# Storing the A22 forms with A11 and A12, and moving the first half's weight sums to one up block earlier

## The chip, the core and the metric

The kernel runs on one core of a Trainium2 chip. The metric is device time in microseconds (us) of the whole program; the time before is the median of three runs, 831.94 us (831.66 to 832.31). The engines are named as the profile names them: PE multiplies matrices, PEld is its weight load, DVE (VectorE) and POOL (GpSimd) do elementwise work, ACT (ScalarE) copies and scales, SP (SyncE) only issues transfers. POOL and ACT issue transfers too, each in the order of its own instruction stream.

## The reference

```python
def reference(q, k, v, w1, w2, w3, w_out):
    scores = scale * q @ k.T                      # per batch (8) and head (8), 576 x 64
    ret = (scores * Dmat) @ v                     # Dmat: gamma**(i-j) for i >= j, else 0
    x = ret.transpose(0, 2, 1, 3).reshape(4608, 512)
    a = x @ w1                                    # 512 x 1024
    b = x @ w2                                    # 512 x 1024
    h = a * b @ w3                                # 1024 x 1024
    return h @ w_out                              # 1024 x 512
```

Everything is float32 on the chip; the float64 inputs of the weights are converted in the kernel. `w3 @ w_out` is multiplied out once.

## The kernel before

**Tiling.** The 8 batches are taken in 4 pairs, each pair in 5 chunks of the sequence (one of 64 rows, four of 128), so there are 20 attention chunks `g`; `NC` is 5. An attention chunk costs PE the products `sc` (scores), `pm`-by-`ld_v` and `xps` and `st` (state). Its q and k come either as whole tiles that PE transposes (`tp`), or in 32 x 32 blocks: 16 small transfers for q and 16 for k (`load_blocks`, L171), a scaling of q on POOL (`scale_blocks`, L181), and block transposes on DVE (`front_blocks`, L190). The tokens are also cut into 12 blocks `m`, each of 2 x 192 tokens.

**Up blocks.** `up(i, n, fp)` multiplies one token block by one quarter `fp` of w1 and w2 with Strassen's seven products. Quarters 0 and 1 lie in half 0 of the weights (`wA[0]`, `wS[0]`), quarters 2 and 3 in half 1. An up block has 28 matmuls, four for each product, named here by its weight form: A11, S2, S3, S1, A22, then A12 added onto the bank of A11 (`p1`), then S4 added onto the bank of S1 (`p5`). DVE adds a product into the sum tile `c` in five calls of `plus` (L533): of S2, of S3, of `p5`, of A22, and of `p5` again after S4. The third of them has to have read `p5` before S4 may be added onto it. ACT copies `p1` into `c` at the start (L546) and once more later (L561); `c` has one buffer, so L546 of a block waits for L566, which multiplies the block before out of `c`. After its add, each `plus` takes one item off the list `aside` and then one off the list `spread` and runs them on the spot. So an item on `spread` stands on DVE between two of these adds.

**Weight forms.** From token block 4 on, `up2` uses a second level of Strassen on the weights. Each half `h` has 7 outer forms, each of which has 7 inner forms. In place on `wA[h]` and `wS[h]`, DVE makes the inner sums with two instructions each (L891: one on `wA` with 1024 columns, one on `wS` with 768): S3 in the place of A21; S2 = A22 - S3 in the place of A22; S1 = S2 + A11 in the place of A11; S4 = A12 - S2 in the place of A12. The forms are stored to `kept[h]` in device memory (`send`: L901 four transfers from `wA`, L904 one or L907 two from `wS`) and loaded again, one outer form at a time, into a ring for `up2` (`next_forms`, L961). A piece of `send` is named by its place `lo` in the 14 x 128 columns of a form, the column block `m`, and the row block `c` or `None` for both. A place may be overwritten only when its store has landed.

**Order before.** The instructions of each engine run in the order of the program text. `weight_forms(h, False)[2]()` at L1187 stores A11 and A12 on POOL's queue, at `g` = 5 for half 0 and at `g` = 6 for half 1. Then, from L1203, four up blocks of token block 3 and what stands between them are put on the list of work: up 0, up 1, `forms[0]` (S3 sum and store of S3 with A22 of half 0, on POOL's queue), up 2, `later` (two empty items), `forms[1]` (S2, S1, S4 sums and the store of S1, S4 and S2, on SP's queue), up 3, `flush`, `forms[2]` (S3 sum and store of S3 with A22 of half 1), `flush`, then the `down` blocks, which multiply `ab` by `w3 @ w_out`. A form entry extends `spread`; `flush` runs what is left on it. Up 0 and up 1 read `wA[0]`, up 2 and up 3 read `wA[1]`, which is why the sums of half 0 can be made from the end of up 1 on.

In this document, "up 0" to "up 3" are these four blocks, "down 1" is the `down` on blocks (1,0) and (1,1) that follows them, and "plus 1" to "plus 5" are the five L533 adds of a block in order. Before the change, the items run as follows: in up 2, plus 1 takes the S3 sum and plus 2 its store; in up 3, plus 1 takes `front_blocks` of q and an empty item, plus 2 an empty item, plus 3 `front_blocks` of k and the S2 sum, plus 4 a sum for `down` (L614) and the S1 sum, plus 5 another (L618) and the S4 sum; then come L566, the store of half 0 on SP, the S3 sum of half 1 and its store.

Of the kernel before, what the change touches and what calls it, by code (L numbers as in the profile page):

```python
# [13 lines left out]
ALU = mybir.AluOpType  # L14
# [5 lines left out]
def kernel(  # L20
# [20 lines left out]
    P = 128  # L41
# [16 lines left out]
    QC = CV // 2  # L58
# [28 lines left out]
    def load(g, names, engine=nc.sync):  # L87
        i, c = divmod(g, NC)
        sz = sizes[c]
        src = {"k": k, "q": q, "v": v}  # L90
        for nm in names:
            t = pools["ld"].tile([P, 2 * H, D], F32, tag="ld_" + nm, name="ld_" + nm)
            engine.dma_start(
                t[:sz], src[nm][2 * i:2 * i + 2, :, starts[c]:starts[c] + sz, :].rearrange("b h p d -> p (b h) d"))
            live[nm, g] = t
# [27 lines left out]
    for c in (0, slice(1, NC)):  # L123
        n = short if c == 0 else P
# [11 lines left out]
    wA = [wp.tile([P, 2, 2, KD // 2, CV], F32, tag=f"wA{h}", name="wA") for h in halves]  # L136
    wS = [wp.tile([P, 3, 2, 2, 2, P], F32, tag=f"wS{h}", name="wS") for h in halves]
# [22 lines left out]
    def load_blocks(g, nm):  # L160

        i, c = divmod(g, NC)
        n = sizes[c] // BL
        t = pools["ld"].tile([P, 2 * NP, P // BL, BL], F32, tag="ld_q", name="bl_" + nm)
        src = {"k": k, "q": q}[nm][2 * i:2 * i + 2].rearrange("b (p a) s d -> a (b p) s d", a=2)
        for a in range(2):
            for f in range(D // BL):
                part = (a * (D // BL) + f) * BL
                for m in range(n):
                    s0 = starts[c] + m * BL  # L170
                    nc.sync.dma_start(t[part:part + BL, :, m, :],  # L171
                                      src[a, :, s0:s0 + BL, f * BL:(f + 1) * BL].rearrange("m r x -> r m x"))
        live["bl_" + nm, g] = t
# [11 lines left out]
    def front_blocks(g, names="kq"):  # L185
        c = g % NC
        n = sizes[c] // BL
        for nm in names:
            dst = pools["fr"].tile([P, 2, NP, P], F32, tag=nm + "T", name=nm + "T", bufs=1 if nm == "k" else 2)
            nc.vector.transpose(  # L190
                dst[:, :, :, :sizes[c]].rearrange("p b m (n x) -> p (b m) n x", x=BL),
                live["bl_" + nm, g][:, :, :n, :])
            live[nm + "T", g] = dst

    def scale(g, nm, scalar=False, engine=nc.gpsimd):
        c = g % NC
        sz = sizes[c]
        t, gam = live[nm, g], {"q": gq, "v": gk}[nm]
        t = t[:sz].rearrange("p (b h) d -> p b h d", b=2)
        if scalar:  # L200
            for h in range(H) if scalar is True else scalar:
                nc.scalar.mul(t[:, :, h, :], t[:, :, h, :], gam[:sz, c, h:h + 1])
            return
        engine.tensor_tensor(
            out=t, in0=t, in1=gam[:sz, c].unsqueeze(1).unsqueeze(3).to_broadcast([sz, 2, H, D]), op=ALU.mult)

    def front(g, names="kq"):
        c = g % NC
        sz = sizes[c]
        for nm in names:  # L210
            src = live[nm, g]
            dst = pools["fr"].tile([P, 2, NP, P], F32, tag=nm + "T", name=nm + "T",
                                   bufs=1 if nm == "k" and g >= NC else 2)
            for b in range(2):
                tp = acc.tile([P, NP, P], F32, tag="acc", name="tp")
                for p in range(NP):
                    h = b * H + 2 * p
                    nc.tensor.transpose(tp[:, p, :sz],  # L218
                                        src[:sz, h:h + 2, :].rearrange("p a d -> p (a d)"),
                                        ident[:sz, :sz])  # L220
                nc.scalar.copy(dst[:, b, :, :sz], tp[:, :, :sz])
            live[nm + "T", g] = dst
# [349 lines left out]
    aside, owed, spread, beside, loads = [], [], [], [], []  # L572
# [256 lines left out]
    todo = [(0, 1, 2), (0, 0, 3), (0, 1, 3)] + [(0, 2, fp) for fp in range(NQ - 1)]  # L829
# [38 lines left out]
    todo = [(down, (0, 0), (0, 1)), (down, (0, 2), (1, 2))]  # L868
# [9 lines left out]
    kept = [hbm.tile([len(NAMES), P, FORM], F32, tag=f"kept{h}", name="kept") for h in halves]  # L878

    def weight_forms(h, second):  # L880

        engine = nc.sync if second else nc.gpsimd

        wa, ws = wA[h].rearrange("p r j c n -> p (r j) c n"), wS[h]

        def tt(out, in0, in1, op):
            def both():
                for w in (wa, ws):
                    o, x, y = (w[:, :, c, m * QC:(m + 1) * QC] if w is wa else w[:, :, m, :, c, :]
                               for m, c in (out, in0, in1))  # L890
                    nc.vector.tensor_tensor(out=o, in0=x, in1=y, op=op)  # L891
            return both

        def send(pieces):
            for lo, m, c in pieces:
                n = 2 * P if c == 1 else 4 * P
                for a in range(4):
                    f, r = divmod(a, 2)
                    x = wA[h][:, r, :, :, m * QC + f * P:m * QC + f * P + P]
                    x = x.rearrange("p j c n -> p (j c) n") if c is None else x[:, :, c, :]  # L900
                    engine.dma_start(kept[h][a, :, lo:lo + n].rearrange("p (g n) -> p g n", n=P), x)  # L901
                to = kept[h][4:7, :, lo:lo + n].rearrange("a p n -> p a n")
                if c is None:
                    engine.dma_start(to, wS[h][:, :, m].rearrange("p a j c n -> p a (j c n)"))  # L904
                else:
                    for j in range(2):
                        engine.dma_start(to[:, :, j * P:(j + 1) * P], wS[h][:, :, m, j, c, :])  # L907

        if second:
            return [tt((1, 1), (1, 1), (1, 0), ALU.subtract), tt((0, 0), (1, 1), (0, 0), ALU.add),  # L910
                    tt((0, 1), (0, 1), (1, 1), ALU.subtract),
                    lambda: send([(8 * P, 0, None), (12 * P, 1, 1)])]
        return [tt((1, 0), (0, 0), (1, 0), ALU.subtract), lambda: send([(4 * P, 1, None)]),
                lambda: send([(0, 0, None)])]

    def weight_of(slot, nm, w):
        lo = {"A11": 0, "A12": P, "S3": 4 * P, "A22": 5 * P, "S1": 8 * P, "S4": 9 * P, "S2": 12 * P}[nm]
# [245 lines left out]
    for g in first_pair:  # L1163
        n = (1, 1, 2, 2)[g - NC]
        if not in_blocks[g + 2]:
            load(g + 2, "k")
            load_blocks(g + 2, "q")
        scale(g + 1, "v")
        if not in_blocks[g + 1]:
            front(g + 1, "k")  # L1170
            front_blocks(g + 1, "q")
        half = (n + 1) // 2
        if in_blocks[g + 1]:
            scale_blocks(g + 1)
            work(n - 1)
            aside.extend([lambda: front_blocks(g + 1, "q"), lambda: None, lambda: front_blocks(g + 1, "k")])
            work(1)
            while aside:
                aside.pop(0)()
            half = 0  # L1180
        if in_blocks[g + 2] and g + 2 < 2 * NC:
            load_blocks(g + 2, "q")
            load_blocks(g + 2, "k")
        work(half)
        if g < NC + 2:

            weight_forms(g - NC, False)[2]()  # L1187
        pv(g)()
        load(g + 2, "v", nc.scalar if in_blocks[g + 2] else nc.sync)
        if in_blocks[g + 2] and (g + 2) % NC != NC - 1:  # L1190
            load(g + 2, "k")
        state(g + 1)
        score(g + 1)
        if not in_blocks[g + 2]:
            scale_blocks(g + 2)
        if g == NC + 1:
            list(strassen_tokens(1, 0))
            forms = [(lambda h=h, second=second: spread.extend(weight_forms(h, second)[:None if second else 2]),)
                     for h in halves for second in (False, True)]
            ups = [(up, 1, 0, fp) for fp in range(NQ)]  # L1200

            later = (lambda: spread.extend([lambda: None] * 2),)
            todo.extend([*ups[:2], forms[0], ups[2], later, forms[1], ups[3], (flush,), forms[2], (flush,), (down, (1, 0), (1, 1)),  # L1203
                         (down, (2, 2), (3, 2)), (open_second,), (down, (3, 0), (3, 1))])
        if not in_blocks[g + 1]:
            work(n // 2)
# [27 lines left out]
    for g in range(2 * NC, G):  # L1234
        n = dealt[g - 2 * NC]
# [87 lines left out]
```

## Time and profile before

| what | value |
|---|---|
| median of three runs | 831.94 us |
| the profiled execution's own time | 832.77 us |
| its span | 831.0 us |
| PE busy | 817.5 us, 98% |
| DVE busy | 547.6 us, 66% |
| ACT busy | 291.8 us, 35% |
| POOL busy | 222.3 us, 27% |
| granted PE clock | 0.999 |
| up 2, first matmul to first matmul of up 3 | 296.23 to 305.43 us |
| up 3, first matmul to the `xps` after it | 305.43 to 314.62 us |
| down 1, first matmul to the `xps` after it | 319.54 to 333.41 us |
| first product of `up2` | 365 us |

Busy time is what an engine spent in instructions; a busy PE may still be slower than it could be, since its matmuls are pipelined. Each product in the timeline of PE counts two records for one float32 matmul, so eight records are one product of an up block. In rows of the timeline, the figures are the start, the duration, engine, line, operation, what it writes and reads, the count, and in square brackets the idle time before it with what ended it.

### The profile page before, as it was taken

What the parts mean: (1) busy time and instruction counts of PE and PEld (TensorE: products, weight loads), DVE (VectorE), ACT (ScalarE), POOL (GpSimd) and SP (SyncE); (2) the same over time, 40 slices, a digit from 0 to 9 for tenths busy, and PEclk for the clock granted to TensorE, in tenths of its full rate; (3) what the DMA queues carried; (4) which work ended last, traced back from release to release, by engine and by line L of the source; (5) the groups of instructions that cost most, each with busy time, mean ns of one, the idle gap of its engine ahead of it and who ended that gap; (6) DMA issues with size and microseconds to landing.
All of it is one profiled execution on the core that took longest, in us unless ns stands there. A gap on an engine that the chain in (4) does not pass through costs nothing.

```text
span 831.0 us, 15815 instructions
## 1 busy us (share of the span) xinstructions
PE 817.5 (98%) x6117; PEld 737.0 (89%) x6117; DVE 547.6 (66%) x962; ACT 291.8 (35%) x609; POOL 222.3 (27%) x258
## 2 busy tenths in 40 slices
PE   8999999999999999999999999999999999999998
PEld 8889999744888998889999889998889998899987
DVE  4899999993544568754657755677745667646653
ACT  4787556572021111255443024341034331033300
POOL 1000000001303332125547015565006460045600
PEclk9999999999999999999999999999999999999999
DMA  9995454446237665988786347978245453146401
GB/s 191 226 224 137 79 131 134 117 126 104 99 66 195 113 151 186 266 264 206 200 228 184 92 88 209 240 224 217 56 92 180 163 191 114 36 149 214 141 26 51
DMA packets 196812, 126.96 MB, mean 153 GB/s; under 512 B 157848, under 2 KB 178456, under 8 KB 196736
## 3 DMA queue, kind: packets, MB, share of 16 engines
q1 hardware_dynamic: 168560, 50.40, 29.6%
q0 software_dynamic: 12480, 65.67, 24.3%
q10 hardware_dynamic: 15696, 9.87, 4.5%
q8 instruction: 48, 0.79, 0.4%
q14 instruction: 28, 0.23, 0.1%
HBM read 103.62 MB, written 22.28 MB: 152 GB/s over the span
## 4 chain that ended last, share of the span: by engine, by line
PE 89%; DVE 6%; DMA 2%; issue 1%; SPq 1%; ACT 1%; ACTq 0%; POOL 0%; DVEq 0%; POOLq 0%
PE po L651 24%; PE up L1060 17%; PE up L528 14%; PE seed L1060 13%; PE ps L477 7%; PE xps L299 3%; PE sc L233 3%; PE xps L274 2%; PE tp L218 2%; PE st L255 1%; SPq L171 1%; DVE pm L236 1%; DVE ab L1032 1%; PE idle L131 1%; DMA ld_v<-in_v_dram 1%
## 5 line engine op out<-in xcount | busy, mean ns | idle before, releaser
L651 PE MATMUL po<-w3o,ab 128*128 128x256 f32 x552 | 125.0, 381 | 2.3 <-DVE ot L655 1.0
L651 PEld LDWEIGHTS po<-w3o,ab 128*128 128x128 f32 x552 | 103.7, 190 | 18.9 <-DVE ot L655 2.5
L1065 POOL TENSOR_TENSOR cc<-cc 128x384 f32<-128x384 f32 x112 | 109.3, 1002 | 3.8 <-ACT cc L1083 2.4
L1072 DVE TENSOR_TENSOR cc<-seed,cc 128x384 f32<-128x384 f32 x88 | 48.7, 553 | 69.0 <-PE seed L1060 59.3
L181 POOL TENSOR_TENSOR bl_q<-bl_q,gqs 128x512 f32<-128x512 f32 (+1 forms) x26 | 26.0, 1020 | 185.8 <-DMA bl_q<-in_q_dram 182.3
L1060 PE MATMUL up<-xT,ra 128*128 128x192 f32 x384 | 73.7, 328 | 0.1
L528 PE MATMUL up<-xT,wA 128*128 128x192 f32 x384 | 70.7, 328 | 1.0 <-DVE xT L496 1.0
L236 DVE TENSOR_TENSOR pm<-sc,mask 128x512 f32<-128x512 f32 (+1 forms) x80 | 45.4, 627 | 35.1 <-PE sc L233 35.1
L1072 DVE TENSOR_TENSOR cc<-up,cc 128x384 f32<-128x384 f32 x88 | 48.5, 551 | 30.2 <-PE up L1060 21.8
L533 DVE TENSOR_TENSOR c<-up,c 128x384 f32<-128x384 f32 x80 | 44.1, 552 | 36.7 <-PE up L528 35.7
L651 PE MATMUL po<-wB,forms 128*128 128x256 f32 x288 | 65.4, 379 | 0.7 <-DVE pm L236 0.7
L528 PEld LDWEIGHTS up<-xT,wA 128*128 128x128 f32 x384 | 63.3, 190 | 2.4 <-PE up L528 1.2
L1060 PEld LDWEIGHTS up<-xT,ra 128*128 128x128 f32 x384 | 63.7, 190 | 1.4 <-DMA ra<-kept 0.4
L961 POOL DMA_DIRECT2D ra<-kept x54 | 30.5, 565 | 118.7 <-PE seed L1060 93.8
L651 PEld LDWEIGHTS po<-wB,forms 128*128 128x128 f32 x288 | 54.6, 190 | 8.4 <-DVE pm L236 1.1
L1079 ACT COPY seed<-up 128x384 f32<-128x384 f32 x56 | 25.9, 463 | 100.2 <-PE up L1060 56.6
L477 PE MATMUL ps<-wo,w3T 128*128 128x512 f32 x128 | 55.1, 592 | 0.0
L1060 PE MATMUL up<-ra 128*128 128x192 f32 x288 | 54.7, 326 | 0.0
L477 PEld LDWEIGHTS ps<-wo,w3T 128*128 128x128 f32 x128 | 24.3, 190 | 30.1 <-issue 29.7
L1060 PE MATMUL seed<-e,ra 128*128 128x192 f32 x256 | 50.9, 329 | 0.0
L1060 PEld LDWEIGHTS up<-ra 128*128 128x128 f32 x288 | 48.1, 190 | 0.1
L528 PE MATMUL up<-T,wS 128*128 128x192 f32 x256 | 46.7, 326 | 1.4 <-DVE wS L149 1.4
(134 smaller groups left out, 1479.1 us busy)
## 6 DMA issues: line engine op xcount, KB each, us to landing
ra<-kept POOLq DMA_DIRECT2D x54, 896.0 KB, 4.9
raw<-in_moe_w_dram SPq DMA_DIRECT2D x72, 128.0 KB, 3.0
bl_q<-in_q_dram SPq DMA_DIRECT2D x192, 32.0 KB, 3.3
out_dram<-ot ACTq DMA_DIRECT2D x41, 128.0 KB, 2.3
bl_k<-in_k_dram SPq DMA_DIRECT2D x136, 32.0 KB, 3.5
raw<-in_moe_w_dram SPq DMA_DIRECT2D x16, 256.0 KB, 5.4
ld_k<-in_k_dram SPq DMA_DIRECT2D x8, 512.0 KB, 6.1
raw<-in_moe_w_out_dram SPq DMA_DIRECT2D x32, 128.0 KB, 2.8
```

Source lines behind the costliest of these rows:

```text
L181: nc.gpsimd.tensor_tensor(out=part, in0=part, in1=gqs[:, :, n0:n0 + n].unsqueeze(3).to_broadcast([P, NP, n, BL]), op=ALU.mult)
L233: nc.tensor.matmul(sc[j][:sz, p, :sz], kT[hs, b, p, :sz], qT[hs, b, p, :sz], start=True, stop=True)
L236: nc.vector.tensor_mul(pm[:sz, b, j, :, :sz], sc[j][:sz, :, :sz], mask[:sz, :sz].unsqueeze(1).to_broadcast([sz, NP, sz]))
L477: nc.tensor.matmul(ps, live["w3T", ft][:, g, :], live["wo"][:, g, :], start=(g == 0), stop=(g == KF - 1))
L528: nc.tensor.matmul(ps[:, w, :], a[:, w, r, :], b[:, r, :], start=(new and w == r == 0), stop=(w == r == 1), skip_group_check=True)
L533: nc.vector.tensor_add(c[:, to], ps, c[:, sb])
L651: nc.tensor.matmul(ps[nm], a[A][:, f, :], live["W"][B][:, f, :], start=(f == 0 and not on), stop=(f == NP - 1), skip_group_check=True)
L961: engine.dma_start(ring[n % 3], kept[n % 14 // 7][nm])
L1060: nc.tensor.matmul(ps[:, w, :], weight_of(slot, a, w), B[b], start=(new and w == 0), stop=True, skip_group_check=True)
L1065: nc.gpsimd.tensor_tensor(out=o, in0=o, in1=i, op=ALU.add)
L1072: nc.vector.tensor_add(c[:, j], ps, with_add[:, j])
L1079: nc.scalar.copy(p6, p1)
```

## The change

`weight_forms(h, False)[2]()`, called at `g` = 5 and 6, stores A22 as well as A11 and A12: the new piece `(5 * P, 1, 1)`. What `forms[0]` and `forms[2]` store behind the S3 sum is S3 alone: `(4 * P, 1, 0)`. Both new pieces go by a path of their own in `send`, with four transfers from `wA` of two runs of 128 columns per partition and two from `wS`. In the list of work, `later` adds one empty item in place of two, and `later` and `forms[1]` stand in front of up 2, not behind it. So `spread` holds seven items at the start of up 2: S3 sum, store of S3, an empty one, S2, S1 and S4 sums, and the store on SP's queue.

```diff
             for lo, m, c in pieces:
+                if m == 1 and c is not None and lo < 12 * P:
+                    place = kept[h][:, :, 4 * P:8 * P].rearrange("a p (j c n) -> a p j c n", j=2, c=2)[:, :, :, c]
+                    for a in range(4):
+                        f, r = divmod(a, 2)
+                        engine.dma_start(place[a], wA[h][:, r, :, c, m * QC + f * P:m * QC + f * P + P])
+                    for j in range(2):
+                        engine.dma_start(place[4:7, :, j].rearrange("a p n -> p a n"), wS[h][:, :, m, j, c, :])
+                    continue
                 n = 2 * P if c == 1 else 4 * P
...
-        return [tt((1, 0), (0, 0), (1, 0), ALU.subtract), lambda: send([(4 * P, 1, None)]),
-                lambda: send([(0, 0, None)])]
+        return [tt((1, 0), (0, 0), (1, 0), ALU.subtract), lambda: send([(4 * P, 1, 0)]),
+                lambda: send([(0, 0, None), (5 * P, 1, 1)])]
...
-
-            later = (lambda: spread.extend([lambda: None] * 2),)
-            todo.extend([*ups[:2], forms[0], ups[2], later, forms[1], ups[3], (flush,), forms[2], (flush,), (down, (1, 0), (1, 1)),
+            later = (lambda: spread.append(lambda: None),)
+            todo.extend([*ups[:2], forms[0], later, forms[1], ups[2], ups[3], (flush,), forms[2], (flush,), (down, (1, 0), (1, 1)),
                          (down, (2, 2), (3, 2)), (open_second,), (down, (3, 0), (3, 1))])
```

## The prediction

> **What bounds the kernel now.** I read the page's first part, the share of each engine:
>
> ```profile
> PE 817.5 (98%) x6117; PEld 737.0 (89%) x6117; DVE 547.6 (66%) x962; ACT 291.8 (35%) x609; POOL 222.3 (27%) x258
> ```
>
> PE is busy for 98% of the span, so only its idle time can be won, and only what makes it idle costs. Then I compared windows over one `down` block, from its first matmul to the `xps` behind it: an undisturbed one, and down 1, which follows the four up blocks.
>
> ```profile
> 253.92:266.20 12.28, 12.28 (x60) 10.55 (x62) 5.61 (x10) 0.74 (x2) 8.09 (x8) 1.00 0.68 163
> 319.54:333.41 13.87, 12.82 (x58) 10.39 (x57) 13.39 (x21) 0.75 (x2) 5.07 (x8) 1.00 0.86 286
> ```
>
> The first two figures after a window are its length and PE's busy time. Down 1 takes 13.87 us instead of 12.28, and DVE (fourth figure) is busy for 13.39 of it. PE's timeline tells where:
>
> ```profile
> 327.37 1.99 PE L651 MATMUL po<-wB,forms 128*128 128x256 f32 x8 [0.65 <-DVE pm L236]
> 329.20 1.89 PE L651 MATMUL po<-wB,ab 128*128 128x256 f32 x8
> 331.49 1.99 PE L651 MATMUL po<-w3o,ab 128*128 128x256 f32 x8 [0.40 <-DVE ot L655]
> ```
>
> PE waits for a bank that DVE hasn't emptied (`pm`), then for an add that DVE made late (`ot`). DVE's timeline shows why it is late, and where it still had time:
>
> ```profile
> 302.74 1.87 DVE L533 TENSOR_TENSOR c<-up,c 128x384 f32<-128x384 f32 x3
> 305.63 0.56 DVE L533 TENSOR_TENSOR c<-up,c 128x384 f32<-128x384 f32 x1 [1.02 <-PE up L528]
> 306.29 0.96 DVE L566 TENSOR_TENSOR ab<-c 128x768 f32<-128x768 f32 x1
> 308.30 0.56 DVE L533 TENSOR_TENSOR c<-up,c 128x384 f32<-128x384 f32 x1 [1.05 <-PE up L528]
> 308.78 1.24 DVE L190 STREAM_TRANSPOSE qT<-bl_q 128x1024 f32<-128x1024 f32 x1
> 309.94 0.52 DVE L533 TENSOR_TENSOR c<-up,c 128x384 f32<-128x384 f32 x1
> 310.83 0.56 DVE L533 TENSOR_TENSOR c<-up,c 128x384 f32<-128x384 f32 x1 [0.38 <-PE up L528]
> 313.87 1.25 DVE L190 STREAM_TRANSPOSE kT<-bl_k 128x1024 f32<-128x1024 f32 x1 [2.48 <-DMA bl_k<-in_k_dram]
> 315.04 1.18 DVE L891 TENSOR_TENSOR wA<-wA 128x1024 f32<-128x1024 f32 x1
> 316.14 0.95 DVE L891 TENSOR_TENSOR wS<-wS 128x768 f32<-128x768 f32 x1
> ...
> 326.63 2.48 DVE L236 TENSOR_TENSOR pm<-sc,mask 128x512 f32<-128x512 f32 x4
> ```
>
> DVE is idle for 1.02, 1.05, 0.38 and 2.48 us before 314; from there on three sums (S2, S1, S4) and S3 of half 1 push `pm`, ready on PE at 319.54, to 326.63.
>
> **The moved sums.** One sum costs 2.0 us of DVE: from 315.04 (L891 on `wA`) to 317.01, where the next L533 starts, 1.97; the later two 2.0 each. The change brings S2 and S1 in front of up 3 and S4 behind its plus 1. I run DVE forward from 304.15, the end of the three adds (a pitch of 0.47 from 302.74, the last one overlapping what follows). S2: 2.0, plus 0.5, since POOL's scaling (L181, 302.72 for 2.06) still runs for 0.63: L566 at 282.05 took 1.49 instead of 0.96 when it overlapped the same scaling by 0.67. To 306.65. Plus 5 of up 2, ready at 305.6: 0.47, to 307.12. S1: 2.0, to 309.12. L566: 0.96, and 0.09 until ACT starts (306.29 + 0.96 against the L546 copy at 307.34), to 310.17. That copy holds plus 1 of up 3, since `c` has one buffer: 0.48 and 0.05, to 310.70. Plus 1: 0.47. Transpose of q: 1.16 (308.78 to 309.94), to 312.33. S4: 2.0, to 314.33. Plus 2: 0.47. Plus 3: 0.56, to 315.36, and 0.06 until PE goes on (331.43, end of the `ot` add, to 331.49): **315.42**.
>
> What PE wanted by then stands in its timeline of up 3:
>
> ```profile
> 311.93 1.46 PE L528 MATMUL up<-xT,wA 128*128 128x192 f32 x8
> 313.23 1.46 PE L528 MATMUL up<-xT,wS 128*128 128x192 f32 x8
> ```
>
> The row at 313.23 is S4, added onto `p5`, which plus 3 must have read first. Before, plus 3 ended at 311.39 and the cover was 1.84 us; now PE waits for **2.2 us**. (In the view of waits, PE is held by L533 once before, for 0.5 us: such a wait exists.) A12 at 311.93 needs only the L546 copy, done at 310.65. Bounds: without the overlap with POOL 1.7; with all of POOL's 2.06 beneath the sums 3.8. I take 2.2.
>
> **What it wins.** From 315.4 the transpose of k (its transfer landed by 313.85, so the idle 2.48 is gone) and plus 4 follow, L614 at 0.60, plus 5, L618 at 0.60, L566 at 0.87, S3 of half 1 at 2.0, L620 at 0.61: 315.3 + 1.16 + 0.47 + 0.60 + 0.47 + 0.60 + 0.87 + 2.0 + 0.61 = 322.1. There `pm` starts, 4.5 us sooner. Down 1 starts 2.2 late at 321.75 and wants the bank of the first `pm` 7.1 later (it took 12.28 - 3 x 1.73 in the undisturbed block), at 328.8. Both of its waits go: 13.87 - 12.28 = **1.6 us** won (1.5 or 1.8 by the other two undisturbed blocks, 12.39 from 336.34 and 12.09 from 237.69). The sum is +2.2 - 1.6 = **+0.6 us**.
>
> **The early store of A22.** POOL issues 6 transfers more behind the five at 215.44 (idle afterwards until 257.9: nothing), and 6 more here:
>
> ```profile
> 262.23 3.04 POOL L901 DMA_DIRECT2D kept<-wA  x4
> 265.25 0.75 POOL L904 DMA_DIRECT2D kept<-wS  x1
> 270.12 1.00 POOL L496 TENSOR_TENSOR xT<-xT 128x384 f32<-128x384 f32 x1 [4.12 <-ACT xT L306]
> 271.20 1.00 POOL L496 TENSOR_TENSOR T<-xT 128x384 f32<-128x384 f32 x1
> ```
>
> At 0.75 each they end at 270.5, 0.4 past the start of L496. Its second sum, T2, then ends at 272.6; PE's S2 product of up 0 wants it at 273.39. Cover left: 0.8; cost: nothing. A22 of a half is 4 x 128 + 2 x 192 = 896 KB, 2.6 us at the 350 GB/s moved from 266 to 268; if it delays q and k of the next chunk by that, q's transposes at 284.61 have 1.9 to spare behind the scaling, and k's at 288.45 push adds before an idle stretch of 3.33 (until `pm` at 295.43): nothing. The row shows five issues in 3.8 us, without a wait between them, and landings of 2.6 to 4.5 us. Against this edit speaks a rule of the Trainium skill ("DMA: Bandwidth & Descriptors", Rules for kernel authors and Anatomy of one DMA): move 1 MiB or more at a time, since each transfer issued from GpSimd has a fixed cost of about 2 us beside its bytes. Were that paid one transfer behind the other, six would hold POOL for an estimated 14 us and the kernel would take an estimated 841 us; by the row it is 0.
>
> **Other parts at nothing.** The store of S3 alone has 6 issues for 5: 0.75 more on POOL at 304.73, before 17 us without work there. The store of half 0 on SP starts when S4's sum ends, near 314.3 instead of 322.39; behind it queue loads of k and q that ACT and PE use after 344, so they only get earlier. S2 now overwrites A22, stored 80 us before, and waits for no store; before, half 1 lost 0.51 us of DVE there (335.58), off PE's path. The dropped empty item issues nothing.
>
> The profiled execution took 832.77 for a span of 831.0, and the median is 831.94; I add the sum to the median: 831.94 + 0.6, so **832.6** (0.7 with the pickup of PE's weight loads).
>
> **Rivals.**
>
> *A: no new wait, a gain.* If DVE's chain from 304.15 to plus 3 takes under 9.0 us instead of 11.2, PE never waits, and 1.6 is won: 830.3. For it: DVE had 4.9 us idle there. Against: 2.48 of them lie behind plus 3. Its time lies on the edge of what can be told.
>
> *B: POOL's queue, slower.* The eleven issues might be paced by landings, like SP's: its ten for half 0 took 322.39 to 331.95, 0.96 each. Then POOL is free at 272.8, T2 ends at 274.8, and PE waits 1.4: 834.0. It decides from 0.88 us an issue on ((271.3 - 266.0) / 6). Against: the five took 0.75.
>
> *C: the sums don't move.* If S2 must also wait for the store of S3 beside it (interleaved in the same rows), it starts when that lands: 304.73 + 4.5 of issue + 4 to 5.5, so 313 to 315 instead of 304.15, and PE waits 9 to 10 us more: 842. Against: the two lie in different columns, and an overwrite has to wait only for a store that reads what it overwrites. No row of before has such neighbours in flight at once, so a small chance stays.
>
> *D: the wait is paid twice.* Tiles get other PSUM banks once the order changes; if down 1 then waits for another late bank, only the 2.2 remain: 834.1. Against: `pm` is 4.5 us sooner.
>
> **Chances.** Forecast 0.54, A 0.15, B 0.15, C 0.06, D 0.10. This kernel's measurement can tell about 0.2%, 1.66 us, from no change: below 830.28 is faster, above 833.60 slower. Faster: two thirds of A, 0.10. Slower: B, C, D and 0.06 of the forecast's upper end (2.2 growing to 3.8), 0.37. Same: 0.53. The forecast's own range is 831.8 (1.7 - 1.8) to 834.2 (3.8 - 1.5). The range reaches down to A and up past B, D and that end: 830.3 to 835.0; left out are the lower half of A, C, and D with the wait at its dearest, some 0.16.
>
> **What would show it.** Right: in PE's timeline an idle stretch of some 2 us before the last product of up 3, ended by L533, and down 1 in 12.1 to 12.4 us with no wait for `pm`; L891 rows directly behind plus 4 and plus 5 of up 2; eleven POOL stores ending by 271. Wrong: plus 3 done before 313.2 (A), L496 after 271.3 (B), an L891 waiting for a store in up 2 (C), a wait left in down 1 (D).

## The result, and the profile after

The changed kernel took 834.08 us (median of 22 runs, 831.45 to 839.16), the kernel before 832.09 beside it (22 runs): a ratio of 1.0027, 95% interval 1.0019 to 1.0034. A second set gave 833.59 against 832.02, 1.0026 (1.0011 to 1.0041). So the change costs some 2 us: inside the range of 830.3 to 835.0 and 1.5 us above the forecast of 832.6. Both intervals lie above 1; the first median is just above the 833.60 from which the prediction calls a result slower, the second just below it.

The profiled execution took 833.71 us for a span of 832.0. The share of each engine hardly moved:

```profile
PE 815.6 (98%) x6117; PEld 735.6 (88%) x6117; DVE 546.6 (66%) x962; ACT 291.6 (35%) x609; POOL 233.6 (28%) x272
```

POOL has 14 instructions more than before, the additional transfers and some 11 us of issuing. To find the loss, PE's timeline of up 3 and down 1 (start, duration, engine, line, what is written and read, idle time before it in brackets):

```profile
310.31 1.46 PE L528 MATMUL up<-xT,wA 128*128 128x192 f32 x8
313.84 2.93 PE L528 MATMUL up<-xT,wS 128*128 128x192 f32 x8 [2.06 <-DVE c L533]
316.70 1.35 PE L274 MATMUL xps<-qT,sb 64*64 64x128 f32 x32
...
327.15 3.62 PE L651 MATMUL po<-wB,forms 128*128 128x256 f32 x16
330.60 1.89 PE L651 MATMUL po<-wB,ab 128*128 128x256 f32 x8
332.33 1.89 PE L651 MATMUL po<-w3o,ab 128*128 128x256 f32 x8
```

The wait that was forecast is there, before the last product of up 3 and ended by `plus` (L533). What wasn't forecast stands behind it: that product takes 2.93 us where its neighbour takes 1.46, and the `xps` behind it 1.35 instead of 1.10. Down 1 has neither of the waits it had before. The windows over the same stretch show why the product is slow (length, then busy time of PE, PEld, DVE, ACT and POOL with counts, granted clock of PE, DMA share, GB/s):

```profile
311.60:313.84 2.24, 0.18 (x3) 0.01 (x1) 2.14 (x5) 0.48 (x1) 0.00 (x0) 1.00 0.54 164
313.84:316.70 2.86, 2.86 (x9) 2.42 (x9) 2.13 (x3) 0.00 (x0) 0.00 (x0) 0.50 1.13 367
316.70:317.98 1.28, 1.28 (x33) 1.11 (x33) 1.18 (x3) 0.00 (x0) 0.00 (x0) 0.78 1.05 388
317.98:321.86 3.88, 3.88 (x68) 3.59 (x64) 3.88 (x5) 1.20 (x4) 1.60 (x3) 1.00 0.78 229
321.86:334.15 12.29, 12.29 (x59) 10.56 (x57) 6.15 (x12) 0.74 (x2) 4.28 (x7) 1.00 1.18 267
```

After 2.24 us in which PE did almost nothing, the granted clock is 0.50 for the next 2.86 us and 0.78 over the 1.28 behind that; only then is it 1.00 again. The last row is down 1 in 12.29 us, against 13.87 before.

DVE's timeline answers to the chain that the prediction ran forward by hand:

```profile
298.05 2.23 DVE L891 TENSOR_TENSOR wA<-wA 128x1024 f32<-128x1024 f32 x1
...
301.08 1.87 DVE L533 TENSOR_TENSOR c<-up,c 128x384 f32<-128x384 f32 x3
302.87 1.30 DVE L891 TENSOR_TENSOR wA<-wA 128x1024 f32<-128x1024 f32 x1
...
305.42 1.21 DVE L891 TENSOR_TENSOR wA<-wA 128x1024 f32<-128x1024 f32 x1
...
308.97 0.56 DVE L533 TENSOR_TENSOR c<-up,c 128x384 f32<-128x384 f32 x1 [0.60 <-ACT c L546]
309.44 1.23 DVE L190 STREAM_TRANSPOSE qT<-bl_q 128x1024 f32<-128x1024 f32 x1
310.60 1.18 DVE L891 TENSOR_TENSOR wA<-wA 128x1024 f32<-128x1024 f32 x1
311.70 0.95 DVE L891 TENSOR_TENSOR wS<-wS 128x768 f32<-128x768 f32 x1
312.57 1.21 DVE L533 TENSOR_TENSOR c<-up,c 128x384 f32<-128x384 f32 x2
...
321.35 2.47 DVE L236 TENSOR_TENSOR pm<-sc,mask 128x512 f32<-128x512 f32 x4
```

The four L891 rows on `wA` begin the sums S3, S2, S1 and S4. S2 starts at 302.87, directly behind plus 4 of up 2 (the last of the three adds at 301.08), so it waits for no store. Plus 2 and plus 3 come behind S4, and with them PE goes on. `pm` starts before down 1 does, and the last wait is gone.

POOL's stores at chunk 6 (the first two rows A11 and A12, the next two A22, then the first work behind them):

```profile
260.28 3.04 POOL L909 DMA_DIRECT2D kept<-wA  x4
263.30 0.75 POOL L912 DMA_DIRECT2D kept<-wS  x1
264.04 2.83 POOL L900 DMA_DIRECT2D kept<-wA  x4
266.87 1.50 POOL L902 DMA_DIRECT2D kept<-wS  x2
268.50 1.00 POOL L496 TENSOR_TENSOR xT<-xT 128x384 f32<-128x384 f32 x1
```

Eleven issues take 8.1 us, 0.71 to 0.76 each, and L496 follows directly. The 2 us of fixed cost per transfer that the Trainium skill ("DMA: Bandwidth & Descriptors", Anatomy of one DMA) states is not paid one transfer behind the other here.

So the profile of after shows a loss of 2.2 (the wait), 1.5 (the product) and 0.2 (`xps`), and a gain of 1.6. Its span is only 1.0 longer than that of before, mainly because this execution came to the `st` of chunk 7 at 267.35 and that of before at 268.97; over all the profiles below that start lies between 267.35 and 269.69, so only stages are compared here, not starts. Not every execution has the half clock, either: the second profile of the change, below, has the same wait without it. A second cost shows only across runs.

### The profile page after: what moved, and what is told of

It reads as the page before. It is cut to its first block, busy times and chain, and to the rows that moved or that the text cites. A ratio compares the mean times of both kernels' runs of the same rounds, so it can differ in the third digit from the quotient of the medians.

```text
span 832.0 us, 15840 instructions
## 1 busy us (share of the span) xinstructions
PE 815.6 (98%) x6117; PEld 735.6 (88%) x6117; DVE 546.6 (66%) x962; ACT 291.6 (35%) x609; POOL 233.6 (28%) x272
## 4 chain that ended last, share of the span: by engine, by line
PE 88%; DVE 5%; DMA 3%; issue 1%; SPq 1%; ACT 1%; ACTq 0%; DVEq 0%
PE po L651 25%; PE up L1068 17%; PE up L528 15%; PE seed L1068 13%; PE ps L477 7%; PE xps L299 4%; PE sc L233 3%; PE xps L274 2%; PE st L255 1%; DMA ld_q<-in_q_dram 1%; PE tp L218 1%; SPq L171 1%; DVE ab L1040 1%; DMA gk<-decay_k_dram 1%; DVE pm L236 1%
## 5 line engine op out<-in xcount | busy, mean ns | idle before, releaser
L533 DVE TENSOR_TENSOR c<-up,c 128x384 f32<-128x384 f32 x80 | 44.0, 551 | 35.7 <-PE up L528 34.5
```

The costliest lines, as they stand in the source:

```text
L533: nc.vector.tensor_add(c[:, to], ps, c[:, sb])
```

## The experiments

Two theories were set against each other. **Order**: all that is lost, is lost by moving the sums, as a wait in up 3 and the clock behind it; the additional stores cost nothing. **Two costs**: the order costs its wait, and the additional store of A22 at `g` = 6 costs time too, by delaying loads on SP's queue. Each edit below is one against the changed kernel, unless it says otherwise.

**Stores alone** (the list of work as before):

```diff
-            later = (lambda: spread.append(lambda: None),)
-            todo.extend([*ups[:2], forms[0], later, forms[1], ups[2], ups[3], (flush,), ...
+            later = (lambda: spread.extend([lambda: None] * 2),)
+            todo.extend([*ups[:2], forms[0], ups[2], later, forms[1], ups[3], (flush,), ...
```

> A22 stored with A11 and A12, S3 alone behind its sum, but the sums in their old places. Theory (all of the loss is the wait of PE before the last product of up 3, with the half clock after it): no wait there, down 1 still in about 13.9 us with its waits for pm and ot, ratio 1.000 (0.999 to 1.001). Rival (the early stores on POOL's queue cost): the ratio keeps most of 1.0027, 1.0015 or more, and up 0 starts its second product late.

Measured: 832.39 us, ratio 1.0004 (0.9994 to 1.0014). Down 1 takes 12.28 us with no wait, though the sums are where they were. So the gain that the prediction gave to the moved sums comes with the stores alone. DVE's timeline:

```profile
312.36 1.25 DVE L190 STREAM_TRANSPOSE kT<-bl_k 128x1024 f32<-128x1024 f32 x1 [0.37 <-DMA bl_k<-in_k_dram]
```

The blocks of k for chunk 9 end DVE's wait at 312.36 instead of 313.87. Their issues end at the same time (309.4 in both), but the last of them lands sooner: at most 3.4 us from issue to landing, against 5.8 before. What changed beside them is the store at 305, which has lost A22: from 300 to 314 the core moved 1.56 MB instead of 2.49. With 1.6 us won and the total unchanged, something else must have been lost. PE's timeline has it:

```profile
293.77 1.15 PE L255 MATMUL st<-ld_v,ld_k 128*64 128x64 f32 x32 [0.54 <-DMA ld_k<-in_k_dram]
```

The state product of chunk 8 waits for its k, a load of 512 KB (L93) that SP issues behind 32 small loads of blocks.

**S4 behind plus 4 of up 3**, the rest of the change kept:

```diff
+            def split_forms():
+                s = weight_forms(0, True)
+                spread.extend([*s[:2], *[lambda: None] * 3, *s[2:]])
+
+            split = (split_forms,)
...
-            todo.extend([*ups[:2], forms[0], later, forms[1], ups[2], ...
+            todo.extend([*ups[:2], forms[0], later, split, ups[2], ...
```

> The change with one sum moved back: S4 behind plus 4 of up 3 instead of plus 1; S2 and S1 stay in up 2. Theory: plus 3 comes 2.0 us sooner, near 311.2 by the clock of the changed kernel's profile, so PE waits 0.0 to 0.3 before the last product of up 3, its clock stays at 1.00, and down 1 takes 12.3: 1.4 to 1.6 us below before, ratio 0.9981 to 0.9985. Rival (stores, or banks dealt anew, cost): 1.000 or above.

Measured: 832.33, 1.0003 (0.9992 to 1.0014), not the 0.9981 to 0.9985 of the theory of the order. The wait in up 3 is gone with the sum that stood in front of plus 2 and plus 3, and 1.8 us of the change's loss with it. `st` again waits for `ld_k`, 0.35 us, and down 1 takes 12.28.

**PE kept busy in the wait**, to take the half clock out and leave the wait:

```diff
+        if i == 1 and fp == NQ - 1:
+            keep_busy(9)
         product(p5, "S4", "B22")
```

> The change with 9 idle matmuls (128 x 128, into a spare bank) before the last product of up 3, so that PE works while it waits for plus 3. Theory: the wait of 2.2 us stays, but the granted clock after it is 1.00, the last product takes 1.4 us instead of 2.9 and the xps after it 1.04 instead of 1.28: 2.2 - 1.6 = 0.6 to 0.8 us above before, ratio 1.0007 to 1.0010, and less scatter. Rival (the slow last product comes from something else, the bank or the transfers beside it): ratio stays at 1.0027.

Measured: 835.39, 1.0047 (1.0033 to 1.0061). The last product took 1.47 us at a full clock, but `st` waited 2.02 us for `ld_k`, and a new wait stands between down 2 and down 3. This run can't price the clock.

**S2 in up 2, S1 in front of the transposes of k, S4 behind plus 4**, to fill DVE's idle 2.48 us:

```diff
+            def split_forms():
+                s = weight_forms(0, True)
+                none = [lambda: None]
+                spread.extend([s[0], *none * 3, s[1], *none, *s[2:]])
+
+            split = (split_forms,)
...
-            todo.extend([*ups[:2], forms[0], later, forms[1], ups[2], ...
+            todo.extend([*ups[:2], forms[0], later, split, ups[2], ...
...
-            aside.extend([lambda: front_blocks(g + 1, "q"), lambda: None, lambda: front_blocks(g + 1, "k")])
+            aside.extend([lambda: front_blocks(g + 1, "q"), lambda: None,
+                          lambda: (spread.pop(0)() if g == NC + 3 else None, front_blocks(g + 1, "k"))])
```

> The stores of the change; S2 behind plus 4 of up 2, S1 behind plus 3 of up 3 and ahead of k's transposes (the place where DVE waited 2.48 us for k), S4 behind plus 4 of up 3. Theory: one sum fits ahead of plus 3 (cover 1.84 and 2.45 idle for 2.5), S1 fits into the wait for k, so no wait in up 3 and none for pm in down 1: 1.5 us below before, ratio 0.9980 to 0.9985, the same as with S4 alone moved back or up to 0.3 us better. Rival: no gain, 1.000.

Measured: 832.3, 1.0011 (0.9997 to 1.0025): no gain. Its profile shows the second cost at its dearest, in PE's timeline:

```profile
290.98 1.97 PE L299 MATMUL xps<-pm,ld_v 128*64 128x128 f32 x32
295.22 1.15 PE L255 MATMUL st<-ld_v,ld_k 128*64 128x64 f32 x32 [2.27 <-DMA ld_k<-in_k_dram]
296.30 3.44 PE L233 MATMUL sc<-qT,kT 64*128 64x128 f32 x32
```

PE is idle for 2.27 us, and the `sc` behind it takes 3.44 us where it takes 2.06 undisturbed: the clock falls here as well. (This execution took 835.21 us, 2.9 above the median of its kernel.) Why the load is late stands in SP's timeline. That of the kernel before has 16 loads of q blocks for chunk 8 and, behind 16 of k blocks left out here, the load of its k (`ld_k`):

```profile
266.12 12.68 SPq L171 DMA_DIRECT2D bl_q<-in_q_dram  x16
...
286.79 0.40 SPq L93 DMA_DIRECT2D ld_k<-in_k_dram  x1
```

SP's timeline of this run has the same two rows later and longer:

```profile
265.69 14.70 SPq L171 DMA_DIRECT2D bl_q<-in_q_dram  x16
...
288.38 0.40 SPq L93 DMA_DIRECT2D ld_k<-in_k_dram  x1
```

The 16 loads of q share the transfers with POOL's eleven stores and take 14.70 us instead of 12.68. All behind them moves: `ld_k` is issued 1.6 us later though the burst began 0.4 sooner. Before, it landed 5.0 us after its issue, at 291.8, and `st` wanted it at 293.21: a cover of 1.4 us. Here the landing itself took 6.7 us (the view of DMA issues); in the three profiles with the longest waits it took 6.1 to 6.7, in the others with stores at 6 between 4.6 and 5.1. Why it varies isn't known.

**Both halves' early stores at `g` = 5**, on three orders: that of the change, that of S4 behind plus 4, and that of before (stores alone). Nothing of the computation differs; the eleven stores of half 1 follow those of half 0, where SP has no such burst (POOL issues the 22 from 214.64 to 230.94 in the third of the kernels; SP's bursts of q end at 208.7 and begin again at 234.4).

```diff
-        if g < NC + 2:
-            weight_forms(g - NC, False)[2]()
+        if g == NC:
+            for h in halves:
+                weight_forms(h, False)[2]()
```

> The change with the early stores of both halves at g = 5, where POOL and the transfers have idle time, and none at g = 6. Theory 2 (the loss has two parts: the wait of 2.2 us before the last product of up 3 with the half clock after it, and a late load of k for chunk 8, whose `st` waits 0.3 to 2.3 us because the stores at g = 6 slow the q and k loads on SP's queue): `st` at 293 waits for nothing, the wait before the last product stays, down 1 in 12.3; ratio 1.0005 to 1.0020, below the change's 1.0027. Theory 1 (the first part alone): unchanged at 1.0027.

> S4 behind plus 4 of up 3, and both halves stored early at g = 5. Theory 2: no wait for k at `st`, none in up 3, down 1 in 12.3: 1.5 us below before, ratio 0.9978 to 0.9988. Theory 1: no difference from the same order with stores at g = 6, which gave 1.0003.

> The new stores alone, sums in their old places, both halves at g = 5. With stores at g = 6 this gave 1.0004 and down 1 took 12.28, since the transfers of k for chunk 9 landed 1.5 us sooner beside a smaller store of S3. Theory 2: that gain of 1.6 us stays and the wait at `st` goes: ratio 0.9978 to 0.9990. Theory 1: 1.000.

Measured: with the order of the change 832.31, 1.0002 (0.9993 to 1.0011); with S4 late 830.3, 0.9978 (0.9969 to 0.9988); with the order of before 830.53, 0.9977 (0.9968 to 0.9986). Each is lower than its partner with stores at `g` = 6, by 1.8 (1.3 by the change's second set), 2.0 and 1.9 us, and the last two beat both kernels. SP's timeline of the third:

```profile
265.25 9.38 SPq L171 DMA_DIRECT2D bl_q<-in_q_dram  x16
274.72 7.79 SPq L171 DMA_DIRECT2D bl_k<-in_k_dram  x16
282.61 0.40 SPq L93 DMA_DIRECT2D ld_k<-in_k_dram  x1
```

With no store beside them the 16 loads take 9.38 us, and `ld_k` is issued almost 10 us ahead of `st` (292.34). The median of the first is below what either theory gave for it. In its profile PE still waits in up 3:

```profile
314.71 1.57 PE L528 MATMUL up<-xT,wS 128*128 128x192 f32 x8 [1.13 <-DVE c L533]
```

Here the wait is 1.13 us and no half clock follows. So the 1.8 us between this kernel and the change aren't all the late load: the two profiles of the change have 0 and 0.2 us of that, and lose 1.0 and 2.3 us more in up 2 and up 3. The other two pairs have no wait in up 3, and theirs is the difference that prices the stores at 6. The order of the change costs 2.0 us against S4 late (832.31 and 830.3).

**The kernel before with a second store**: six transfers of A22 of half 1 more at `g` = 6, to a place that nobody reads.

```diff
+        if g == NC + 1:
+            for a in range(4):
+                f, r = divmod(a, 2)
+                nc.gpsimd.dma_start(extra[a], ...)
+            for j in range(2):
+                nc.gpsimd.dma_start(extra[4:7, ...], ...)
```

> The kernel before, with A22 of half 1 stored once more, at g = 6, to a place that nobody reads; everything else as before. Theory 2: the 16 q loads on SP at 266 take 14.2 to 14.7 us instead of 12.7, the load of k for chunk 8 is issued 1.5 to 2 us later, `st` waits 0.3 to 2.3 us at 293, and nothing is won in down 1: ratio 1.0010 to 1.0035. Theory 1: 1.000.

Measured: 832.5, 1.0009 (0.9997 to 1.0020); the median alone shows no loss. Its profile does (an execution of 834.61 us, 2.1 above the median). The 16 loads of q take 15.03 us, and PE's timeline shows the wait:

```profile
294.58 1.15 PE L255 MATMUL st<-ld_v,ld_k 128*64 128x64 f32 x32 [2.33 <-DMA ld_k<-in_k_dram]
295.66 3.53 PE L233 MATMUL sc<-qT,kT 64*128 64x128 f32 x32
```

Two windows behind that wait show the clock (the figure before the last two):

```profile
294.58:296.00 1.42, 1.42 (x38) 1.35 (x39) 0.00 (x0) 0.23 (x1) 0.00 (x0) 0.99 1.32 240
296.00:299.12 3.12, 3.12 (x32) 2.90 (x28) 1.29 (x2) 0.35 (x1) 0.72 (x1) 0.50 0.73 98
```

The kernel before, with nothing but these stores, gets the wait for `ld_k` and the half clock. It gets something back: with PE 4 us late, the blocks of k for chunk 9 are there in time, and down 1 takes 12.28 instead of 13.87. So up to 1.6 us of a late `st` can be won back as long as down 1 has its waits, and none once they are gone, as in the change.

**Once more: PE kept busy, with both stores at `g` = 5**, and the change itself for a second profile.

```diff
+        if i == 1 and fp == NQ - 1:
+            keep_busy(5)
         product(p5, "S4", "B22")
```

> The change with both early stores at g = 5 (832.31 us), and five idle matmuls (some 1.1 us of PE by the 2.0 us that nine took before) ahead of the last product of up 3, where PE was idle for 1.13 us in the profile of that kernel and for 2.06 us in that of the change. If the half clock after the wait is part of what the new order costs in most runs, the time falls by 0.5 to 1.5 us, to 830.8 to 831.8. If the order costs the wait alone, the matmuls lie within the wait where it is long and lengthen it where it is short: 832.2 to 833.0. The last product of up 3 should take 1.46 to 1.57 us at a clock of 1.00 in both cases.

> The change itself once more, for a second profile. If the late load of k for the chunk behind up 1 is a cost of the change, the product st on ld_v and ld_k there waits for its transfer in this profile, for 0.3 to 2.3 us, which it did not in the first; the wait before the last product of up 3 is 1.1 to 2.2 us, and the median is 833.3 to 834.5. If only the order costs, st does not wait, as in the first profile.

Measured: 833.99 us, 1.0023 (1.0015 to 1.0032), for the first, more than either theory gave. Up 2 and up 3 together take what they took without the matmuls (19.79 and 19.80 us); what is longer is elsewhere. One part is the same as in the first try, where it stands at 353.73:

```profile
350.10 5.45 PE L653 MATMUL po<-w3o,ab 128*128 128x256 f32 x24 [1.46 <-DVE spare L657]
```

The tile that the idle matmuls write takes one of the seven PSUM banks, so the products behind it presumably fall on other banks, and here on one that DVE empties late. That last link was not tried by itself. Another part, a wait of 1.29 us for a load of stored forms at 402.84, stands only in this profile, the slowest of the kernel's executions. How much the half clock costs in most runs stays open. Part of it can be read from the granted clock, a mean over the whole span that is on record for each run. A stretch of 3.4 us at half clock lowers it by an estimated 0.002 (1.7 us of 832). Of the 34 runs of the change 17 have 0.999 or more, with a median of 833.46 us; the kernel before has 54 such runs of 82, with a median of 832.04. So some 1.4 us of the loss is there without such a stretch. The other 17 of the change have a median of 834.85.

The change's second profile shows the wait in up 3 again, without the half clock:

```profile
314.81 1.57 PE L528 MATMUL up<-xT,wS 128*128 128x192 f32 x8 [2.13 <-DVE c L533]
```

`st` came 0.2 us later after the `st` before it than in the kernel before, less than expected and too little to carry the theory alone. The stages of all profiles, from the starts in PE's timelines, hold both costs (us; 24.24, 3.02 and 18.39 is the undisturbed pace):

| kernel | `st` of chunk 7 to `st` of chunk 8 | to up 2 | up 2 and up 3 | down 1 |
|---|---|---|---|---|
| before | 24.24 | 3.02 | 18.39 | 13.87 |
| change | 24.24 | 3.02 | 22.09 | 12.29 |
| change, second profile | 24.44 | 3.06 | 20.80 | 12.28 |
| stores alone | 24.96 | 3.07 | 18.39 | 12.28 |
| S4 late | 24.76 | 3.06 | 18.40 | 12.28 |
| PE kept busy | 26.43 | 3.07 | 20.40 | 12.28 |
| S1 in the gap | 26.69 | 4.45 | 18.61 | 12.29 |
| before, second store | 26.75 | 4.54 | 18.62 | 12.28 |
| change, both at 5 | 24.24 | 3.02 | 19.80 | 12.29 |
| S4 late, both at 5 | 24.24 | 3.02 | 18.40 | 12.29 |
| stores alone, both at 5 | 24.25 | 3.01 | 18.40 | 12.28 |
| both at 5, PE kept busy | 24.24 | 3.02 | 19.79 | 12.28 |

The first two columns are late only with eleven stores at `g` = 6, in six of seven such profiles; with both at 5 they never are. Over the seven, columns one and two together are late by 1.7 us on average (0, 0.24, 0.77, 0.56, 2.24, 3.88, 4.03), near the 1.9 and 2.0 us between the medians of the two pairs without a wait in up 3. The third column is long only with S4 in front of plus 3.

## Why the prediction came out 1.5 us low

**The wait in up 3: right in place and cause.** 2.2 us were forecast; the two profiles of the change show an idle stretch of 2.06 and 2.13. From the S1 sum on the hand-run chain holds to about 0.1 us. That its end fits, too, is partly luck, for the first two terms miss in opposite directions: the row of the three adds ends at 304.61 (302.74 + 1.87), not at 304.15, and S2 took 2.1 us, not 2.5, as only 0.2 us of POOL's scaling of q was left beside it. The chain also starts from a row of before in which the sum of S3 (299.68, 2.27 us) ran beside POOL's scaling of v (L204); where it hardly does, the wait is half as long. In the kernel of the change with both stores at 5, that v landed 4.3 us after its issue, against 5.3 and 5.6 in the change, L204 came sooner in up 2, the L891 of S3 at 299.86 takes 1.28 us, against 2.23 and 2.30, and the wait is 1.13.

**What follows that wait: not foreseen.** In one of the two profiles of the change the wait brought a half clock, 1.7 us more than the two products' usual time. It belongs to this step's price, but not in every execution: the step, as a term, is 1.4 to 3.7 us by the third column of the table, and 1.8 to 2.0 by the medians with and without S4 late.

**Down 1: right in size, half right in cause.** 1.6 forecast, 1.58 measured in each of the kernels. But the stores alone win it, by letting the k of chunk 9 land sooner. I had credited it to the moved sums, which, being paid for with a wait, weren't needed.

**The early store of A22 at nothing: the step that failed.** The forecast worked out that q and k of the next chunk might come 2.6 us late and checked that their transposes have that to spare. It looked only at the loads whose traffic collides. The load that mattered stands behind them on SP's queue: `ld_k` of chunk 8 with 1.4 us of cover. The runs show 0 to 2.5 us of wait there and up to 1.5 of half clock behind it. Taking the stores to `g` = 5 is worth 1.9 and 2.0 us on the two orders that have no wait in up 3, so this item, put at nothing, is large enough for the 1.5 us that the forecast missed. It isn't the whole of the miss: the two profiles of the change show only 0 and 0.2 us of it, and in one of them the half clock. How the 2 us of the change divide in most runs stays open.

**The rivals.** *A* (no wait) needed a chain under 9.0 us and fell. *B* (POOL paced by landings) fell: L496 starts at 268.50, before 271.3. The row it was priced from holds eleven issues (4, 1, 4 and 2), not ten, so 0.87 us each and not 0.96, and its own sum would give an estimated 833.1; and the five stores it was weighed against landed 2.6 to 5.5 us after their issue, not 2.6 to 4.5. That the result lies at 834.0 all the same is chance: POOL's stores did hold up PE, but through SP's queue and not POOL's own, and the order cost its share. *C* fell with S2 directly behind plus 4. *D* fell: no wait is left in down 1.

## What to carry to other kernels

When transfers are added, find each queue that has transfers in the air at that time, and follow that queue past the loads that collide to the first one with a tight deadline: a delay beyond the cover of that load is what the transfers cost. A store that can be made at any time belongs where no burst of small loads runs: the same stores one chunk sooner turned a loss of 2 us into nothing, and with the sums in their old order into a gain of 1.4. A part that is credited with a gain should be taken out alone: here the half of the change that was meant to win it only cost.

## What was unexpected of the hardware

A gap of some 2 us on PE can cost more than itself. After idle stretches of 2.06, 2.27 and 2.33 us, the granted clock fell to about 0.50, at once in one case and 1.4 and 1.5 us after work had resumed in the other two, for some 3.4 us; after 2.02 and 2.13 us it stayed at 1.00. The length of the gap doesn't decide alone: near the kernel's start, a gap of 2.70 us (to 41.83, "PE kept busy") was followed by 0.50 at once, and one of 2.98 us (to 42.27, "change, both at 5") by 1.00. The Trainium skill ("TensorE: Matmul & The Clock Gate", Part 1: The HAM clock gate) gives a window of about 3.4 us that runs freely, and half clock after at least one idle window. The length of the slow stretch agrees with it; that a gap shorter than one window can set it off is measured here, against what that part of the page states.
